# Slot attention with a split-precision feed-forward: laying the slot weights' maxima along the rows by two DMAs through device memory

## The chip, the cores and the metric

The kernel runs on one core of a Trainium2 chip. The metric is the device time of one execution in microseconds (us); lower is better. A core has TensorE (PE; PEld is its weight loads), VectorE (DVE), ScalarE (ACT), GpSimd (POOL) and SyncE (SP), each with an in-order queue of its own, and DMA engines that move data for all of them. SyncE issues all of this kernel's DMAs.

## The reference

Eight batches of eight heads, 576 positions, head size 64, 32 memory slots. A softmax of phi along the positions gives the slot weights, these sum k and v into 32 slots, q attends to the slots, and a feed-forward with an exact gelu follows.

```python
a = phi - np.max(phi, axis=2, keepdims=True)
a = np.exp(a)
a = a / (np.sum(a, axis=2, keepdims=True) + 1e-09)
k_m = np.einsum('bhsm,bhsd->bhmd', a, k)
v_m = np.einsum('bhsm,bhsd->bhmd', a, v)
scores = scale * np.matmul(q, k_m.transpose(0, 1, 3, 2))
...
attn_out = np.matmul(attn, v_m)
...
h = x @ w_in
g = 0.5 * h * (1.0 + erf(h * inv_sqrt2))
return g @ w_out
```

x is the attention's output, 4608 rows of 512; w_in is 512 by 2048, w_out 2048 by 512. Everything is float32.

## The kernel before

**The main stream.** Slots times w_in are folded first: per batch, U = (v slots) times w_in (pu, L441), so that the hidden layer of a batch is h = U times the attention weights. The 2048 hidden units go in 16 slices f of 128. For each slice of a batch TensorE makes h in two halves of 288 positions (L680, 12 products in the trace), ACT applies gelu from PSUM (gf, L690 for the first half; L692 and tails, L693, for the second), DVE splits gf into a high part gh and a rest gl (L155, L699), and TensorE projects with w_out (L712, three products for each of four accumulators, 12 products). The projection of a slice stands in TensorE's queue behind h of the next slice. h lives in two PSUM banks, one for each half, so the next slice's half waits for gelu of the same half. A step is one half. Batches 0 and 1 run slices 0 to 7, then 8 to 15, by turns; batches 2 to 7 run all 16 at once. After each odd batch the last 64 positions of two batches are projected together (tacc).

**The preparation of a batch** is laid between these steps, far ahead. For batch b from 2 on it needs the slot weights in two layouts. With slots on the partitions phi is loaded (Lphi, L240), DVE takes the maxima along the positions, negated (nm, L292, two columns of 128 values), and ACT makes the exponentials only for their sums (L298). With positions on the partitions phi is loaded again as aT (Lphin, L335 for 512 positions and L340 for the last 64). Here the maxima are needed along the free axis, the same row on every partition. The old way is a diagonal matrix (dg, L348: the identity times the column nm) and a product of ones with it (L355), which leaves in PSUM the row of maxima on every partition; for batches 2 and 3 in a pair of banks of its own, pn, for later ones in a free half of the pair tn that holds the transposes of the last batch's slots (L407). Then DVE adds the row to aT (L362) and ACT takes exponentials in place (L366, the 64 positions and the 512 apart). The products of aT with k and v (pk or psc, L383) give the slots, five position pieces for each of two head groups, each piece with its own kv load (L251, eight buffers). km (L397) scales them, L407 transposes, kT is copied by ACT, and score and pu follow (L441).

**What sets the order.** The first part up to batch 1 is written out by hand (START). From there `put(t, ...)` gives pieces a step at which they are due, and the program's scheduler reorders each engine's queue under the rule that a piece comes no earlier than four steps ahead of its due time. `prepare(b, t, tn)` sets the due steps: phi's load at t, the maxima at t + 2, the diagonal at t + 3, the load of aT at tn - 1, sums and exponentials at tn + 1. The pair of PSUM banks (pool ps_at, one buffer) is shared by pn, tn, pk, psc and pu; the next one waits until the readers of the last are done. ACT's exponential and gelu are in different tables, and each change of table is a load.

Of the kernel before, what the change touches and what calls it, by code (L numbers as in the profile page):

```python
# [9 lines left out]
F32 = mybir.dt.float32  # L10
# [4 lines left out]
ALU = mybir.AluOpType  # L15
# [57 lines left out]
def slot_attention_gelu_ffn(  # L73
# [28 lines left out]
    nc = tc.nc  # L102
    P = 128
    B, G, _, S = phiT.shape
# [19 lines left out]
    const = ctx.enter_context(tc.tile_pool(name="const", bufs=1))  # L124
    gs = ctx.enter_context(tc.tile_pool(name="gs", bufs=2))
    sb = ctx.enter_context(tc.tile_pool(name="sb", bufs=2))
    ps_acc = ctx.enter_context(tc.tile_pool(name="ps_acc", bufs=1, space=bass.MemoryType.PSUM))
    ps_h = ctx.enter_context(tc.tile_pool(name="ps_h", bufs=2, space=bass.MemoryType.PSUM))
    ps_at = ctx.enter_context(tc.tile_pool(name="ps_at", bufs=1, space=bass.MemoryType.PSUM))
# [4 lines left out]
    ones = one.to_broadcast([P, P])  # L134
    ident = const.tile([P, P], F32, name="ident")
# [12 lines left out]
    st = {"engine": None}  # L148
# [10 lines left out]
    def tile_of(key, make):  # L159
        if key not in st:  # L160
            st[key] = make()
        return st[key]

    def banks(*k):

        return tile_of(
            k, lambda: ps_at.tile([P, G, FB], F32, tag="at", name="_".join(map(str, k)))
        )
# [10 lines left out]
    def load_w(k, f):  # L179
        at = slice(f * P, (f + 1) * P)  # L180
        if k == 0:
            i = nc.sync.dma_start(
                raw_of(f)[:, 0].rearrange("p (c n) t -> p c (n t)", c=ND),
                w_in[:, at].bitcast(I32).rearrange("(c p) n -> p c n", p=P),
            )
        else:
            i = nc.sync.dma_start(
                raw_of(f)[:, 1].rearrange("p n t -> p (n t)"), w_out[at, :].bitcast(I32)
            )

        if "gate" in st:
            tc.add_manual_dep(i.ins, st["gate"].ins.name, edge, reason="U first")
# [148 lines left out]
            aT[P - TL :, full].rearrange("p g n -> p (g n)"), phiN[b, full * P :]  # L341
        )

    def a_diag(b):

        dg = st["dg", b] = sb.tile([P, G, P], F32, tag="dg", name=f"dg_{b}", bufs=1)
        for g in range(G):
            nc.vector.tensor_scalar_mul(dg[:, g], ident, st["nm", b][:, g : g + 1])  # L348

    def a_cols(b):  # L350

        pn = banks("tn", b - 1) if b > 3 else banks("pn", b)
        pn = st["pn", b] = pn[:, 1, : G * P].rearrange("p (g n) -> p g n", g=G)
        for g in range(G):
            nc.tensor.matmul(pn[:, g], ones, st["dg", b][:, g], start=True, stop=True)  # L355

    def a_nat(b):

        aT, pn, full = st["aT", b], st["pn", b], S // P
        xs = ((aT[P - TL :, full:], P - TL, 1), (aT[:, :full], 0, full))  # L360
        for x, r, n in xs:
            nc.vector.tensor_tensor(  # L362
                x, x, pn[r:].unsqueeze(1).to_broadcast([P - r, n, G, P]), op=ALU.add
            )
        for x, _, _ in xs:
            nc.scalar.activation(x, x, AF.Exp)  # L366
# [392 lines left out]
    def tail_evict(b):  # L759
# [7 lines left out]
    pieces = {  # L767
        "Lphi": load_phi, "Lkv": load_kv, "Lkv0": load_kv0, "Lq": load_q,
        "Lwi": lambda f: load_w(0, f), "Lwo": lambda f: load_w(1, f),
        "Lphin": load_phin, "dg": a_diag, "pn": a_cols, "anat": a_nat, "amax": a_max, "aexp": a_exp, "anorm": a_norm,  # L770
        "at": a_T, "atc": a_Tc, "slots": slots, "km": slots_m,
        "slotsT": slots_T, "kT": k_T,
        "n_score": score_n, "n_max": n_max, "n_sub": n_sub, "n_exp": n_exp, "n_sum": n_sum,
# [23 lines left out]
    def put(t, *xs):  # L797
        for x in xs:
            if x not in done:
                plan.append((t, len(plan), x))  # L800
# [6 lines left out]
    n = 2 * NF  # L807

    def prepare(b, t, tn):

        put(t, *(f"Lphi.{b}.{g}" for g in range(G)))
        put(t + 2, *(f"amax.{b}.{g}" for g in range(G)))
        put(t + 3, f"dg.{b}")
        put(tn - 1, f"Lphin.{b}")

        put(tn + 1, f"anat.{b}", *(f"aexp.{b}.{g}" for g in range(G)), f"anorm.{b}")


    for b, t in ((2, T2), (3, 65)):
        prepare(b, t, t + 5)  # L820
        put(t + 1, *(f"Lkv.{b}.0.{c}" for c in range(NC)))
        put(t + 5, f"pn.{b}")
        put(t + 9, f"slots.{b}.0", f"km.{b}.0")
        put(t + 9, *(f"Lkv.{b}.1.{c}" for c in range(NC)))
        put(t + 11, f"slots.{b}.1", f"km.{b}.1")
# [3 lines left out]
    for b in range(3, B):  # L829
        t = n * (b - 1)  # L830
        tn = {3: 78, 4: 91}.get(b, t - n + 24)
        put(tn, f"slotsT.{b}")
        if b + 1 < B:
            prepare(b + 1, tn - 8, tn)
            put(tn, f"pn.{b + 1}")
        put(tn, f"kT.{b}")
    for b in range(2, B):
        t = n * (b - 1)
# [17 lines left out]
    for f in range(NF):  # L856
        t = 2 * at_step[0, f]
# [86 lines left out]
```

## Time and profile before

| | |
|---|---|
| Time, median of 3 runs | 734.56 us (734.01 to 736.58) |
| Span of the profiled execution, first to last instruction | 733.8 us |
| Chain that ended last: TensorE's share | 90% |
| L355 products in the trace | 24 (12 in the program), 3.6 us busy |
| L348 diagonals on DVE | 12, 3.1 us busy |
| ACT table loads in the groups L298, L366, L571, L690, L692 | 12, 8, 13, 30, 4 at 1.28 us |
| DMA | 65.15 MB, 26.5% of the engines' time |

The profiled execution's span lies 0.2 us under the fastest run and 0.8 us under the median, so the two can be laid side by side to within about a microsecond. In the trace each float32 product of the program is two instructions. A row of the chain gives a start, a length and what the time went to; a row of a timeline gives start, length, engine, line, operation and tiles, with the idle time before it and what ended it in brackets. Batch numbers count from 0.

### The profile page before, as it was taken

The numbers are of one execution on the slowest core, as the hardware profiler recorded it, in microseconds if no ns is written. First come the engines' busy times: TensorE is split into PE (matmuls) and PEld (weight loads), VectorE is DVE, ScalarE is ACT, GpSimd is POOL, SyncE is SP. The second block draws the span as 40 slices with busy tenths as digits, with TensorE's granted clock in tenths as the row PEclk, the third lists the DMA queues.
The fourth block names the chain that finished last, engine by engine and source line by source line (L and its number), as shares of the span: only waits on it lengthen the run. The fifth ranks groups of instructions, "written<-read, shape, count | busy, mean of one in ns | idle before, by whom it ended". The sixth has DMA issues, their size and how long they took to land.

```text
span 733.8 us, 12179 instructions
## 1 busy us (share of the span) xinstructions
PE 708.0 (96%) x4958; PEld 578.8 (79%) x4958; DVE 394.7 (54%) x686; ACT 346.6 (47%) x713; POOL 48.7 (7%) x45
## 2 busy tenths in 40 slices
PE   5888899999999999999999999999999999999997
PEld 4666687886788887888888878888788888888886
DVE  2799999844674347535454364533643346333323
ACT  4577886782427847524752247432431234232210
POOL 1043243300000000000000000000000000000000
PEclk7589999999999999999999999999999999999999
DMA  9964163305432433051101521050101110010002
GB/s 296 320 213 140 58 220 104 120 1 187 137 105 71 150 112 95 23 216 62 33 1 59 193 62 33 1 205 25 37 1 59 47 33 1 0 58 1 1 1 72
DMA packets 42584, 65.15 MB, mean 89 GB/s; under 512 B 2848, under 2 KB 24992, under 8 KB 42528
## 3 DMA queue, kind: packets, MB, share of 16 engines
q1 hardware_dynamic: 42528, 64.37, 26.5%
q8 instruction: 39, 0.64, 0.4%
q14 instruction: 17, 0.14, 0.1%
HBM read 54.92 MB, written 9.44 MB: 88 GB/s over the span
## 4 chain that ended last, share of the span: by engine, by line
PE 90%; DVE 3%; ACT 2%; issue 2%; DMA 1%; SPq 0%; POOL 0%; ACTq 0%; POOLq 0%
PE acc L712 47%; PE h L680 27%; PE tacc L712 6%; PE pu L441 4%; PE psc L383 1%; DMA kv<-kv 1%; PE psc L441 1%; PE psc L458 1%; PE pk L383 1%; DVE raw L208 1%; DVE y L207 1%; DVE gl L699 0%; DVE s L482 0%; DVE wo_lo L230 0%; PE tn L355 0%
## 5 line engine op out<-in xcount | busy, mean ns | idle before, releaser
L680 PE MATMUL h<-p_hi,U 128*128 128x288 f32 x1024 | 206.4, 300 | 4.5 <-ACT tails L693 3.3
L712 PE MATMUL acc<-wo_hi,gh 128*128 128x512 f32 x512 | 203.0, 396 | 0.0
L712 PE MATMUL acc<-wo_lo,gh 128*128 128x512 f32 x512 | 201.2, 393 | 0.0
L712 PE MATMUL acc<-wo_hi,gl 128*128 128x512 f32 x512 | 201.0, 394 | 0.0
L680 PEld LDWEIGHTS h<-p_hi,U 128*128 128x128 f32 x1024 | 164.4, 189 | 26.0 <-issue 6.7
L690 ACT ACTIVATE gf<-h 128x288 f32<-128x288 f32 x128 | 52.9, 413 | 231.3 <-issue 167.7
L155 DVE CAST gh<-gf 128x512 fp32r<-128x512 f32 x108 | 46.7, 432 | 199.8 <-ACT gf L692 199.6
L712 PEld LDWEIGHTS acc<-wo_hi,gh 128*128 128x128 f32 x512 | 96.1, 188 | 33.2 <-DVE gh L155 7.5
L712 PEld LDWEIGHTS acc<-wo_hi,gl 128*128 128x128 f32 x512 | 95.9, 188 | 22.7 <-DVE gh L155 0.8
L680 PE MATMUL h<-p_lo,U 128*128 128x288 f32 x512 | 110.1, 296 | 0.4 <-DVE p_lo L536 0.4
L712 PEld LDWEIGHTS acc<-wo_lo,gh 128*128 128x128 f32 x512 | 96.1, 188 | 17.4 <-issue 0.4
L699 DVE TENSOR_TENSOR gl<-gf,gh 128x512 fp32r<-128x512 f32 x128 | 89.9, 703 | 10.1 <-ACT gh L155 1.6
L680 PEld LDWEIGHTS h<-p_lo,U 128*128 128x128 f32 x512 | 83.3, 189 | 1.8 <-DVE p_lo L536 1.0
L692 ACT ACTIVATE gf<-h 128x224 f32<-128x224 f32 x128 | 45.6, 356 | 41.9 <-PE h L680 41.8
L643 DVE TENSOR_TENSOR U<-pu,U 128x1024 fp32r<-128x1024 f32 (+2 forms) x39 | 40.0, 1024 | 14.9 <-ACT U L155 14.9
L690 ACT ACT_TABLE_LOAD x30 | 38.5, 1283 | 10.2 <-issue 6.3
L155 ACT CAST U<-pu 128x1024 fp32r<-128x1024 f32 (+2 forms) x39 | 33.8, 867 | 19.8 <-PE pu L441 19.8
L441 PE MATMUL pu<-w_in_sb,kT 64*32 64x512 f32 (+2 forms) x624 | 37.0, 531 | 2.5 <-DVE U L643 2.1
L208 DVE SCALAR_TENSOR_TENSOR raw<-raw 128x512 int32<-128x512 int32 (+1 forms) x33 | 36.4, 1104 | 0.3
L693 ACT ACTIVATE tails<-h 128x64 f32<-128x64 f32 x128 | 28.3, 221 | 0.0
L549 DVE STREAM_TRANSPOSE sT<-psc 128x288 f32<-128x288 f32 x28 | 12.1, 463 | 29.8 <-PE psc L383 24.2
L202 ACT ACTIVATE y<-raw 128x512 f32<-128x512 f32 (+1 forms) x33 | 22.9, 693 | 10.8 <-DMA raw<-w_in 7.0
(94 smaller groups left out, 625.8 us busy)
## 6 DMA issues: line engine op xcount, KB each, us to landing
kv<-kv SPq DMA_DIRECT2D x68, 256.0 KB, 4.5
raw<-w_in SPq DMA_DIRECT2D x16, 512.0 KB, 6.4
raw<-w_out SPq DMA_DIRECT2D x16, 512.0 KB, 6.5
out<-o SPq DMA_DIRECT2D x16, 512.0 KB, 2.9
q<-qT SPq DMA_DIRECT2D x14, 576.0 KB, 5.3
phi<-phiT SPq DMA_DIRECT2D x16, 288.0 KB, 5.5
aT<-phiN SPq DMA_DIRECT2D x6, 512.0 KB, 4.6
kv<-kv SPq DMA_DIRECT2D x4, 512.0 KB, 10.1
```

The lines of the kernel that those rows point to most:

```text
L155: return e.copy(dst, src) if e is nc.scalar else e.tensor_copy(dst, src)
L202: nc.scalar.activation(y, high.bitcast(F32), AF.Abs, scale=2.0**16)
L208: nc.vector.scalar_tensor_tensor(low, high, -(2**31), low, op0=ALU.bitwise_and, op1=ALU.bitwise_or)
L383: nc.tensor.matmul(pk[32 * j : 32 * j + 32, w0 * D : (w0 + n) * D], st["aT", b][:rows, c, g, 32 * j : 32 * j + 32], t[:rows, w0 : w0 + n, ...
L441: nc.tensor.matmul(ps[g][M * j : M * j + M], st["kT", b][rows, t, M * j : M * j + M], moving[rows, j, :], start=True, stop=True,)
L643: nc.vector.tensor_sub(u[:, :, 1], st["pu", b, f], u[:, :, 0].bitcast(F32))
L680: i = nc.tensor.matmul(h[:, :HS], u[g][w], x[:, g, :], start=(n == 0), stop=(n == 3 * G - 1))
L690: nc.scalar.activation(gf[:, :HS], h[:, :HS], AF.Gelu)
L692: nc.scalar.activation(gf[:, HS:], h[:, : MAIN - HS], AF.Gelu)
L693: nc.scalar.activation(tails()[:, f, b % 2], h[:, MAIN - HS : HS], AF.Gelu)
L699: nc.vector.tensor_tensor(g_of("gl", b, f), g_of("gf", b, f), g_of("gh", b, f).bitcast(F32), op=ALU.subtract)
L712: nc.tensor.matmul(acc, x, w[:, f, :], start=(first and n == 0), stop=(last and n == 2))
```

## The change

From batch 2 on the diagonal and the product are gone. The column nm is written by a DMA into a tile in device memory (row, two rows of 128), and a second DMA reads these rows back to every partition of a tile in SBUF (nb); DVE adds nb to aT. Both DMAs are issued by SyncE, and the second waits until the first has landed. The preparation of batches 2 and 3 starts one step earlier, and its aT load, sums and exponentials are due one step later.

```diff
+    hbm = ctx.enter_context(tc.tile_pool(name="hbm", bufs=2, space=bass.MemoryType.DRAM))
...
-    def a_diag(b):
-
-        dg = st["dg", b] = sb.tile([P, G, P], F32, tag="dg", name=f"dg_{b}", bufs=1)
-        for g in range(G):
-            nc.vector.tensor_scalar_mul(dg[:, g], ident, st["nm", b][:, g : g + 1])
-
-    def a_cols(b):
-
-        pn = banks("tn", b - 1) if b > 3 else banks("pn", b)
-        pn = st["pn", b] = pn[:, 1, : G * P].rearrange("p (g n) -> p g n", g=G)
-        for g in range(G):
-            nc.tensor.matmul(pn[:, g], ones, st["dg", b][:, g], start=True, stop=True)
+    def a_row(b):
+
+        row = hbm.tile([G, P], F32, tag="row", name=f"row_{b}")
+        nc.sync.dma_start(row.rearrange("g p -> p g"), st["nm", b])
+        nb = st["nb", b] = sb.tile([P, G, P], F32, tag="nb", name=f"nb_{b}", bufs=1)
+        nc.sync.dma_start(nb, row.unsqueeze(0).to_broadcast([P, G, P]))
 
     def a_nat(b):
 
-        aT, pn, full = st["aT", b], st["pn", b], S // P
+        aT, nb, full = st["aT", b], st["nb", b], S // P
...
-                x, x, pn[r:].unsqueeze(1).to_broadcast([P - r, n, G, P]), op=ALU.add
+                x, x, nb[r:].unsqueeze(1).to_broadcast([P - r, n, G, P]), op=ALU.add
...
-        put(t + 3, f"dg.{b}")
+        put(t + 3, f"row.{b}")
...
-        prepare(b, t, t + 5)
+        prepare(b, t - 1, t + 6)
...
-        put(t + 5, f"pn.{b}")
...
-            put(tn, f"pn.{b + 1}")
```

The scheduler lays the queues anew. Three places matter below; the last number of a name is a serial number, and lines of the new kernel differ by a few from the old.

On ACT, where batch 2 is prepared (slices 13 to 15 of batch 0), there stood before:

```order
L298 ACT_TABLE_LOAD
L298 ACTIVATE phi_1626,sm_1769<-phi_1626,nm_1684 128x576
L690 ACT_TABLE_LOAD
L690 ACTIVATE gf_14_1722<-h_0_14_1715 128x288
L692 ACTIVATE gf_14_1722<-h_1_14_1728 128x224
L693 ACTIVATE tails<-h_1_14_1728 128x64
L366 ACT_TABLE_LOAD
L366 ACTIVATE aT_1724<-aT_1724 64x256
L690 ACT_TABLE_LOAD
L690 ACTIVATE gf_15_1763<-h_0_15_1756 128x288
L366 ACT_TABLE_LOAD
L366 ACTIVATE aT_1724<-aT_1724 128x1024
```

and now stands:

```order
L361 ACT_TABLE_LOAD
L361 ACTIVATE aT_1740<-aT_1740 64x256
L685 ACT_TABLE_LOAD
L685 ACTIVATE gf_14_1725<-h_0_14_1718 128x288
L687 ACTIVATE gf_14_1725<-h_1_14_1727 128x224
L688 ACTIVATE tails<-h_1_14_1727 128x64
L361 ACT_TABLE_LOAD
L361 ACTIVATE aT_1740<-aT_1740 128x1024
L685 ACT_TABLE_LOAD
L685 ACTIVATE gf_15_1763<-h_0_15_1756 128x288
L687 ACTIVATE gf_15_1763<-h_1_15_1765 128x224
L688 ACTIVATE tails<-h_1_15_1765 128x64
```

The exponentials of aT have moved ahead by one slice and lie between slices; the second exponential of phi has moved behind slice 15. On DVE the two sums come ahead of gh and gl of slice 13, the 512 positions first. On SyncE the load of aT, which stood right behind phi's, stands behind row, and its tail behind nb.

On SyncE, between the last kv loads of batch 3 (kv_1_3, kv_1_4, numbers 25..) and the loads of batch 4, there stood before:

```order
L251 DMA kv_1_3_2584<-kv 128x512
L251 DMA kv_1_4_2586<-kv 128x512
L251 DMA kv_0_0_2661<-kv 128x512
L251 DMA kv_0_1_2663<-kv 128x512
L251 DMA kv_0_2_2665<-kv 128x512
L285 DMA q_0_2749<-qT 128x4x288
L251 DMA kv_0_3_2667<-kv 128x512
L335 DMA aT_2657<-phiN 128x4x256
```

and now stands:

```order
L241 DMA phi_2454<-phiT 128x576 x2
L252 DMA kv_1_3_2583<-kv 128x512
L348 DMA row_2517<-nm_2501 128x2x1
L252 DMA kv_1_4_2585<-kv 128x512
L252 DMA kv_0_0_2660<-kv 128x512
L252 DMA kv_0_1_2662<-kv 128x512
L350 DMA nb_2519<-row_2517 128x256
L252 DMA kv_0_2_2664<-kv 128x512
L336 DMA aT_2656<-phiN 128x4x256
```

Batch 4's phi, which was issued ahead of all five kv loads of batch 3's second group, now stands ahead of the fourth, row ahead of the fifth, and nb ahead of batch 4's aT. The second phi exponential of batch 3, whose end frees the tile for batch 4's phi, has moved on ACT behind both exponentials of aT and half of the next gelu. On TensorE the first group of five pieces (pk of batch 3) has moved from between the two halves of slice 5 to behind ten products of the projection that follows, and the second group is cut into four pieces and one.

On ACT, in batch 5's slices 11 to 13, where batch 6 is prepared, there stood before (from the copy of kT on):

```order
L155 COPY kT_3769<-tn_3764 128x256
L692 ACTIVATE gf_12_3762<-h_1_12_3771 128x224
L693 ACTIVATE tails<-h_1_12_3771 128x64
L155 CAST p_hi_1_3796<-pT_1_3794 128x576
L366 ACT_TABLE_LOAD
L366 ACTIVATE aT_3739<-aT_3739 64x256
L366 ACTIVATE aT_3739<-aT_3739 128x1024
L690 ACT_TABLE_LOAD
L690 ACTIVATE gf_13_3831<-h_0_13_3824 128x288
L155 CAST U_0_3809<-pu_0_3800 128x2x512
```

and now stands:

```order
L156 COPY kT_3764<-tn_3761 128x256
L361 ACT_TABLE_LOAD
L361 ACTIVATE aT_3736<-aT_3736 64x256
L687 ACT_TABLE_LOAD
L687 ACTIVATE gf_12_3759<-h_1_12_3766 128x224
L688 ACTIVATE tails<-h_1_12_3766 128x64
L361 ACT_TABLE_LOAD
L361 ACTIVATE aT_3736<-aT_3736 128x1024
L156 CAST p_hi_1_3791<-pT_1_3789 128x576
L156 CAST U_0_3804<-pu_0_3795 128x2x512
L685 ACT_TABLE_LOAD
L685 ACTIVATE gf_13_3826<-h_0_13_3819 128x288
```

The two exponentials are apart, with a pair of table loads more between them, and the cast of U has come ahead of slice 13's gelu. Batch 7 reads the same. On TensorE pu, which stood within slice 13's second h, now stands right behind slice 12's h, ahead of a projection, since the banks of tn no longer wait for DVE's sums.

More of the change, by code (lines that the diff above doesn't have):

```diff
@@ L769, in slot_attention_gelu_ffn @@
         "Lwi": lambda f: load_w(0, f), "Lwo": lambda f: load_w(1, f),
-        "Lphin": load_phin, "dg": a_diag, "pn": a_cols, "anat": a_nat, "amax": a_max, "aexp": a_exp, "anorm": a_norm,
+        "Lphin": load_phin, "row": a_row, "anat": a_nat, "amax": a_max, "aexp": a_exp, "anorm": a_norm,
         "at": a_T, "atc": a_Tc, "slots": slots, "km": slots_m,
```

## The prediction

> **What bounds the kernel now.** I read the page first, then the stages, then the chain of waits stage by stage, and last the timelines of ACT, DVE and SyncE's queue where the change puts its hands. The page's first part and the head of its chain:
>
> ```profile
> PE 708.0 (96%) x4958; PEld 578.8 (79%) x4958; DVE 394.7 (54%) x686; ACT 346.6 (47%) x713; POOL 48.7 (7%) x45
> ...
> PE 90%; DVE 3%; ACT 2%; issue 2%; DMA 1%; SPq 0%; POOL 0%; ACTq 0%; POOLq 0%
> ```
>
> The stage table (PE, PEld, DVE, ACT, POOL busy, clock, DMA share, GB/s) has this row for a stretch in which batches 3 and 4 are prepared:
>
> ```profile
> 240.00:310.00 70.00, 70.00 (x582) 56.79 (x581) 37.67 (x69) 46.26 (x79) 0.61 (x2) 1.00 0.27 88
> ```
>
> TensorE is the bound: never idle there, at full clock, and it carries nine tenths of the chain. So an edit counts by what it takes from TensorE's queue or what wait it puts into it; DVE, ACT and the DMA engines have room on average and matter only where TensorE is made to wait.
>
> Around batch 2's maxima the chain, in order of time (start, length, what), reads:
>
> ```profile
> 155.42 1.59 PE h L680 x12
> 157.01 0.44 PE pn L355 x4
> ...
> 161.82 2.77 PE acc L712 x12
> 164.58 0.81 PE h L680 x6
> ...
> 165.42 1.06 ACT L692
> ...
> 166.50 0.36 ACT gf L692
> ...
> 167.02 1.06 PE h L680 x6
> ```
>
> A slice takes 1.59 + 2.77 = 4.36 us on TensorE. The group pn, which the change deletes, lies on the path with 0.44. And there is one real wait: between 164.58 + 0.81 = 165.39 and 167.02 TensorE stands still, 1.6 us, for ACT, which is loading a table.
>
> **The deleted products.** The same chain in the other batches:
>
> ```profile
> 231.30 0.45 PE pn L355 x4
> ...
> 246.37 0.80 PE h L680 x6
> 247.17 1.23 PE pk L383 x40
> ...
> 252.91 1.23 PE pk L383 x40
> ...
> 258.88 0.45 PE tn L355 x4
> ```
>
> and in batches 6 and 7 (two answers):
>
> ```profile
> 366.12 0.46 PE tn L355 x4
> ...
> 366.63 0.36 ACT gf L692
> ...
> 367.15 1.06 PE h L680 x6
> ...
> 376.53 1.59 PE h L680 x12
> ```
>
> ```profile
> 457.19 0.46 PE tn L355 x4
> ...
> 457.69 0.36 ACT gf L692
> ```
>
> In batches 2 and 3 the group stands alone and goes whole: 0.44 + 0.45. In batches 4 and 5 it stands behind the transposes of L407, which stay, and with them the change from one kind of product to the other; I take 0.4 each. In batches 6 and 7 TensorE waits for ACT right behind the group (366.63 and 457.69): without the group it waits 0.46 longer, so nothing. Sum: **-1.7 us**. The diagonals (L348) and the sums with a row from SBUF in place of PSUM are DVE's, which is covered by TensorE; if that cover went, it would be a gain of some tenths a batch.
>
> **The wait at 165.4.** ACT there, as the timeline has it:
>
> ```profile
> 162.40 0.41 ACT L690 ACTIVATE gf<-h 128x288 f32<-128x288 f32 x1
> 162.83 1.28 ACT L366 ACT_TABLE_LOAD   x1
> 164.12 1.06 ACT L366 ACTIVATE aT<-aT 128x1024 f32<-128x1024 f32 x1
> 165.20 1.28 ACT L692 ACT_TABLE_LOAD   x1
> ```
>
> The exponential of aT with its two table loads (1.28 + 1.06 + 1.28 = 3.62) sits between the two halves of slice 15's gelu, and the next slice's second h needs the PSUM bank of the second half. In the new order it sits between slices, and the other exponential of phi goes behind slice 15's whole gelu: both halves are through by 163.2 (162.40 + 0.41 + 0.36) and TensorE wants the bank at 165.4. The displaced phi exponential (two loads and about 1 us) then ends near 166.7, and its gelu is wanted one slice later. **-1.6 us**, provided that DVE's sums come in time. That is the new wait in batch 2, since DVE runs in order and gh and gl of slice 13 stand behind the sums:
>
> ```profile
> 146.09 0.74 DVE L292 TENSOR_REDUCE nm<-phi 128x1 f32<-128x576 f32 x1
> ...
> 154.87 0.43 DVE L155 CAST gh<-gf 128x512 fp32r<-128x512 f32 x1 [2.96 <-ACT gf L692]
> 155.40 0.69 DVE L699 TENSOR_TENSOR gl<-gf,gh 128x512 fp32r<-128x512 f32 x1
> ```
>
> The maxima are there at 146.8. Then SyncE issues row, the large aT load, waits until row has landed (x), issues nb and the tail of aT. No row shows a write of 256 pieces of 4 bytes or a read of one kilobyte by 128 partitions; the nearest are the writes of 128 KB and the loads of 64 KB (KB each, median us to landing):
>
> ```profile
> out<-to SPq DMA_DIRECT2D x8, 128.0 KB, 2.4
> ...
> aT<-phiN SPq DMA_DIRECT2D x6, 64.0 KB, 4.4
> ```
>
> With x = 3, nearest to the write, the last load is issued near 150.5 and lands near 154.9; sum of the tail 0.4, gh 0.43, gl 0.69: 156.4. TensorE wants gl at 156.85 + 2 x 0.23 = 157.3 (three products of a slice's twelve in 2.77). Hidden, with 0.9 us to spare: 0, and one for one beyond x = 3.9. Below, x can't give a gain, since gh waits for gelu at 154.8 anyhow. By the Trainium skill, "DMA: Bandwidth & Descriptors", section "Rules for kernel authors", a strided last dimension becomes one descriptor per element, which speaks against this write. By the same page's section "Anatomy of one DMA" (for GpSimd's path) a small transfer costs about 2.0 us, mostly the write's receipt; with that for x the sum is the same. No run here shows either for this write.
>
> **The queue in batches 3 and 4.** ACT's second phi exponential of batch 3, which frees the tile for batch 4's phi, and how long those two loads take from issue:
>
> ```profile
> 233.15 0.78 ACT L298 ACTIVATE phi<-phi,nm 128x576 f32<-128x576 f32 x1
> ```
>
> ```profile
> DMA to landing us min/median/max: 2.8/3.0/3.1
> ```
>
> That exponential moves behind two more exponentials, two slices and a table load (2 x 4.36 + 1.28 = 10 us), to 243.2. So phi of batch 4 is issued at 244, has landed at 247.5, and its two maxima, with U's subtraction between them, are ready near 249.6. Row goes out behind the load before it, near 250.7, and behind row stands the last kv piece of batch 3, which in the old queue waits for no maximum. It lands 2.5 to 3.7 us later by the kv loads of batch 2:
>
> ```profile
> DMA to landing us min/median/max: 2.5/3.2/3.7
> ```
>
> that is at 253.7 to 254.9. On TensorE the first group of five pieces moves from between the two h to behind ten of the projection's twelve products (246.37 - 0.45 + 2 x 0.80 + 10 x 0.23 = 249.8). The second group, today at 252.91, is cut into four and one, and the one is reached near 254.1 (249.8 + 1.23, two products, a half h, four pieces, the bubbles and half of the next h). So 0 to 0.8 of waiting, I take 0.3, and 0.35 for one more change of the kind of product: **+0.65**. In batch 4 the aT load stands behind nb, which waits for row: issued near 250.7 + x + 0.9, landed about 4.4 later, then DVE's two sums (2.5 times the columns of gl, so 1.7), gh and gl, 2.8 in all: gl is there at 258.8 + x and wanted near 264.6, hidden up to x = 5.8. In batches 5 to 7 row and nb stand ahead of loads that TensorE releases much later, well before their use.
>
> **Batches 6 and 7.** ACT in batch 6 from the copy of kT on:
>
> ```profile
> 367.27 0.39 ACT L155 COPY kT<-tn 128x256 f32<-128x256 f32 x1
> 368.25 0.36 ACT L692 ACTIVATE gf<-h 128x224 f32<-128x224 f32 x1 [0.58 <-PE h L680]
> ...
> 368.61 0.68 ACT L155 CAST p_hi<-pT 128x576 fp32r<-128x576 f32 x1
> 369.30 1.28 ACT L366 ACT_TABLE_LOAD   x1
> 370.60 0.42 ACT L366 ACTIVATE aT<-aT 64x256 f32<-64x256 f32 x1
> 371.80 1.06 ACT L366 ACTIVATE aT<-aT 128x1024 f32<-128x1024 f32 x1 [0.79 <-DVE aT L362]
> ...
> 374.48 1.01 ACT L155 CAST U<-pu 128x1024 fp32r<-128x1024 f32 x1
> ```
>
> The new order has a pair of loads more here and the cast of U ahead of slice 13's gelu: 367.27 + 0.39 + 4 x 1.28 + 0.42 + 0.6 (gelu and tails) + 1.06 + 0.68 + 1.01 = 376.55, and 0.41 for gelu, 376.96. TensorE wants slice 14's h at 376.4 in the timeline, 376.5 with pu moved ahead of a projection: 0.45 of waiting and 0.1 for the move, **+0.55 in each, +1.1**. In batch 5 the same exponentials join another under one table and save a pair, off the path.
>
> **Sum.** -1.7 - 1.6 + 0.65 + 1.1 = -1.55. The profiled execution's span is 733.8; less 1.55 that is 732.2. The median of the runs, 734.56, lies 0.8 above the span, so **733.0 us**.
>
> **Rivals.** 0.5% is 3.7 us, about what a measurement of this kernel can tell from no change.
>
> Clean removal, 730.5 (0.16): no new wait in batches 3, 6 and 7, and the 0.46 of the last two is gained as well (-1.7 - 1.6 - 0.8 = -4.1). For it: ACT is idle over half the time and could run ahead. Against: the sum of ACT's pieces above.
>
> No gain, 735 (0.14): DVE's wait for the landing delays ACT's exponential in batch 2, so that the table wait only moves; -1.7 + 0.65 + 1.1 and some tenths more in batch 3. So the change would not do to the time what it does to the queue. For it: the spare 0.9 us is small.
>
> Slow trip through device memory, 739 (0.10): TensorE stands still behind gl in batch 2 and in batch 4. It decides from x = 3.9 in batch 2 and from x = 5.8 in batch 4; at x = 8 it costs 4.1 + 2.2, so -1.55 + 6.3 = +4.75, or 739; at x = 7 it is 737. The page's rule on 4-byte pieces would act here. Against it: 16 pieces to each of 16 engines are few, and all writes of the table land within 3.5 us.
>
> The forecast has 0.60. Faster by over 0.5% (under 730.9): most of the clean removal, 0.14; slower (over 738.2): most of the slow trip, 0.09; within 0.5%: 0.77. The range leaves out the ends of both: 730.2 to 737.4.
>
> **What would show it.** Right: no pn or tn from dg in the chain; no wait for ACT tails in batch 2; a wait of some tenths for ACT gf in batches 6 and 7; DVE's aT sums waiting for DMA nb or aT in batch 2 without TensorE behind them; row landing in 2 to 4 us. Wrong: TensorE waiting for DVE gh or gl near 157, for kv near 252 by more than 1 us, or for nothing at all in batches 6 and 7.

## The result: 2.5% slower

The changed kernel takes 754.16 us (median of 4 runs, 753.8 to 754.6) where the kernel before takes 735.57 beside it (4 runs): a ratio of 1.0251, 95% interval 1.0234 to 1.0267. That is 18.6 us, and 21 above the forecast. The profiled execution's span is 752.3, against 733.8.

The first part of the page of the changed kernel: TensorE is busy 4 us longer though it has fewer products; the two stages below show where from.

```profile
PE 712.1 (95%) x4934; PEld 579.5 (77%) x4934; DVE 393.1 (52%) x674; ACT 346.6 (46%) x713; POOL 47.6 (6%) x45
```

What TensorE waited for, and what SyncE's queue waited for, in the whole execution (total us, times, longest). Of the first, 8.0 us are new and fall in batch 3 (the kernel before waited 5.2 us for kv, all of it before 150 us); the second is new, and the third is the second DMA behind the first:

```profile
PE pk L378 <- DMA kv<-kv: 8.5, 3, 5.2
PE acc L707 <- DVE gh L156: 6.3, 1, 6.3
```

```profile
SPq L350 <- DMA row<-nm: 48.0, 6, 9.4
```

The stages (PE, PEld, DVE, ACT, POOL busy, clock, DMA share, GB/s): first 150 to 170 in the kernel before, then the changed kernel. Its second is the one shown in the prediction with TensorE busy for all 70.00 us at clock 1.00:

```profile
150.00:170.00 20.00, 18.36 (x103) 16.07 (x102) 8.55 (x18) 17.31 (x27) 0.03 (x1) 1.00 0.00 1
```

```profile
150.00:170.00 20.00, 13.71 (x68) 11.61 (x67) 6.29 (x9) 11.34 (x17) 0.83 (x1) 0.83 0.36 65
...
240.00:310.00 70.00, 61.07 (x504) 48.34 (x503) 29.97 (x55) 41.00 (x71) 0.61 (x2) 0.93 0.41 101
```

TensorE stands still in both, for 6.3 and 8.9 us, and the granted clock is 0.83 and 0.93 where it was 1.00. To place every microsecond I compare when the first product of the same slice's projection starts in two traces. Differences to the kernel before, in us, by stages of that kernel's time, for the changed kernel and four of the experiments below:

```
stage of before    work there      changed  e2 due times  e6 pairs  e13 blocks  e7 batch 2's due times
  0 to  73         start            +0.8       +1.1         -0.2       -0.3        +0.1
152 to 173         batch 2          +5.7       -1.5         -1.7       +1.2        -1.6
173 to 243         between          -1.0       -0.4         -0.7       -0.8        -0.2
243 to 281         batches 3, 4    +11.2       +0.8         +7.7       +1.5         0.0
281 to 331         batch 5          +0.8        0.0          0.0       +0.1         0.0
331 to 412         batch 6          +0.5        0.0         +0.5       +0.5         0.0
412 to 502         batch 7          +0.6        0.0         +0.5       +0.6         0.0
```

The change touches nothing in the first 73 us; what differs there, up to 1.2 us either way, is scatter of single executions. The loss is in two places.

**Batch 2.** SyncE's queue and the loads around row (KB each, us to landing):

```profile
147.66 0.38 SPq L348 DMA_DIRECT2D row<-nm  x1
148.09 0.47 SPq L336 DMA_DIRECT2D aT<-phiN  x1
156.21 0.34 SPq L350 DMA_DIRECT2D nb<-row  x1
```

```profile
aT<-phiN SPq DMA_DIRECT2D x1, 512.0 KB, 12.6
nb<-row SPq DMA_DIRECT2D x1, 128.0 KB, 5.6
...
row<-nm SPq DMA_DIRECT2D x1, 1.0 KB, 8.5
```

One kilobyte takes 8.5 us to land, and the load issued right behind it 12.6 where the median of these loads was 4.6 before. DVE's timeline shows the rest of the way, and TensorE's the end of it:

```profile
161.91 1.68 DVE L357 TENSOR_TENSOR aT<-aT,nb 128x1024 f32<-128x1024 f32 x2 [9.47 <-DMA nb<-row]
163.62 0.43 DVE L156 CAST gh<-gf 128x512 fp32r<-128x512 f32 x1
```

```profile
164.10 0.80 PE L707 MATMUL acc<-wo_hi,gh 128*128 128x512 f32 x1 [6.29 <-DVE gh L156]
164.69 0.63 PE L707 MATMUL acc<-wo_lo,gh 128*128 128x512 f32 x1
165.12 0.63 PE L707 MATMUL acc<-wo_hi,gl 128*128 128x512 f32 x1
...
167.65 0.39 PE L707 MATMUL acc<-wo_hi,gl 128*128 128x512 f32 x1
167.88 0.40 PE L707 MATMUL acc<-wo_hi,gh 128*128 128x512 f32 x1
```

gh's gelu, on ACT, was done long before:

```profile
155.28 0.35 ACT L687 ACTIVATE gf<-h 128x224 f32<-128x224 f32 x1
```

gh is late because it stands behind the sums in DVE's queue. And the wait costs more than its 6.29 us: the eight products after it start 0.43 us apart and more, the later ones 0.23. The stage table has the granted clock at half there:

```profile
164.10:167.60 3.50, 3.50 (x8) 2.71 (x9) 1.81 (x3) 3.46 (x6) 0.00 (x0) 0.50 0.00 0
```

So TensorE works at about half pace for 3.5 us, which is some 1.6 us more. With the table wait gone (-1.9 from one slice to the next) and the product gone (-0.44) that makes 5.5; measured 5.7.

**Batch 3.** TensorE's timeline among the five pieces of the second group, and the kv loads issued from 256.5 to 258.0, the last two of that group with row between them:

```profile
258.93 0.86 PE L378 MATMUL pk<-kv,aT 128*32 128x128 f32 x24
264.97 0.66 PE L378 MATMUL pk<-kv,aT 128*32 128x128 f32 x8 [5.17 <-DMA kv<-kv]
...
269.50 0.65 PE L378 MATMUL pk<-kv,aT 128*32 128x128 f32 x8 [2.86 <-DMA kv<-kv]
```

```profile
L252 SPq DMA_DIRECT2D kv<-kv x2: 328/866/1403, 256.7 to 257.6; - x2
...
DMA to landing us min/median/max: 8.2/10.0/11.8
```

The load that was issued ahead of row is late too. All five loads of that group in the kernel before:

```profile
L251 SPq DMA_DIRECT2D kv<-kv x5: 328/382/1199, 247.6 to 250.2; - x5
...
DMA to landing us min/median/max: 3.2/3.5/3.8
```

The waits are 8.0 us of this stage's 11.2. Most of the other 3 is half pace again: the granted clock is 0.50 for 10.2 us, in which TensorE is busy for 5.57, so that about 2.8 us more are spent than at full clock.

```profile
263.20:273.40 10.20, 5.57 (x28) 3.98 (x29) 1.47 (x3) 0.47 (x2) 0.30 (x1) 0.50 0.80 139
```

### The profile page after: what moved, and what is told of

Read it like the earlier page. It is cut to its first block, busy times and chain, and to the rows that moved or that the text cites. A ratio compares the mean times of both kernels' runs of the same rounds, so it can differ in the third digit from the quotient of the medians.

```text
span 752.3 us, 12154 instructions
## 1 busy us (share of the span) xinstructions
PE 712.1 (95%) x4934; PEld 579.5 (77%) x4934; DVE 393.1 (52%) x674; ACT 346.6 (46%) x713; POOL 47.6 (6%) x45
## 5 line engine op out<-in xcount | busy, mean ns | idle before, releaser
L378 PE MATMUL pk<-kv,aT 128*32 128x128 f32 (+2 forms) x368 | 14.3, 297 | 13.7 <-DMA kv<-kv 8.5
```

The costliest lines, as they stand in the source:

```text
L378: nc.tensor.matmul(pk[32 * j : 32 * j + 32, w0 * D : (w0 + n) * D], st["aT", b][:rows, c, g, 32 * j : 32 * j + 32], t[:rows, w0 : w0 + n, ...
```

## The experiments

Theory: row's write is slow by its layout in device memory, and loads around it are held up as long; TensorE pays where it waits for one of them. Rivals: the new order of the instructions costs the time (the order); SyncE's queue, which carries row and all the loads, makes it slow (the queue); any trip through device memory beside loads is as slow (the trip).

### The order without the DMAs (e2_schedule)

```diff
-        prepare(b, t, t + 5)
+        prepare(b, t - 1, t + 6)
...
-        put(t + 5, f"pn.{b}")
+        put(t + 6, f"pn.{b}")
```

> The kernel before, with its diagonal and its products, but with the new due times of batches 2 and 3 (everything one step earlier at the front and one later at the end). ACT has the new order there: the exponentials of aT between slices in batch 2, batch 4's phi issued late in batch 3. No DMA through device memory. Theory (the DMAs cost the time): 733 to 736, about the kernel before, with the table wait of batch 2 (1.6 us) gone and some tenths given back in batch 3. Rival (the new order costs the time): 745 or more, with TensorE waiting for kv near 252.

Measured: 735.24, ratio 0.9992 (0.9979 to 1.0005). Batch 2 gains 1.5 us and batch 3 gives 0.8 back, as the table shows. (From one slice to the next the steps are 1.9 and 1.5; two of the expectations below use these.) TensorE waits for no kv between 230 and 300. The order is out: alone it costs nothing.

### Row on another engine's queue (e4_act_row)

```diff
-        nc.sync.dma_start(row.rearrange("g p -> p g"), st["nm", b])
+        nc.scalar.dma_start(row.rearrange("g p -> p g"), st["nm", b])
```

> The changed kernel with row issued by ScalarE's DMA queue in place of SyncE's; nb and all loads stay on SyncE's. If row's 4-byte writes are slow by themselves: row still lands in 8 to 10 us and TensorE still waits about 6 us behind gh in batch 2. Then, if they hold up only what stands behind them in their own queue, the kv loads of batch 3 land in 3 to 4 us, TensorE's 8 us of waiting there goes and the time is about 743; if they hold up the loads of any queue, the kv loads still take 8 us or more and the time stays near 754. Rival (SyncE's queue makes row slow): row lands in 2 to 3 us and the time is near 736.

Measured: 753.32, ratio 1.0247 (1.0222 to 1.0271). Row's landings in this kernel, then those of the three kv loads issued at 257.0 to 257.9, which now have no row in their queue:

```profile
L348 ACTq DMA_DIRECT2D row<-nm x6: 366/366/402, 148.0 to 446.8; - x6
...
DMA to landing us min/median/max: 7.8/8.9/11.3
```

```profile
L252 SPq DMA_DIRECT2D kv<-kv x3: 328/378/1560, 257.0 to 257.9; - x3
...
DMA to landing us min/median/max: 6.8/10.0/10.7
```

A few other instructions change places with this edit, but the losses stand where they stood. The queue is out: row is as slow, and it holds up the loads of another queue about as long. The Trainium skill, "DMA: Bandwidth & Descriptors", section "Issuing engines are not separate DMA queues", says that all issuers' DMAs run on the same 16 engines and interleave; this trace agrees, with 6.8 to 10.7 us for loads that took 3.2 to 3.8.

### The write measured by itself (e1_prices, e8_prices)

Six writes in each, late in the kernel before, each from a fresh copy so that it starts there; the core of three of those in e8_prices:

```diff
+        if k == "A":
+            d = hbm.tile([2, P], F32, tag=name, name=name)
+            nc.sync.dma_start(d.rearrange("g p -> p g"), c[:, :2])
+        if k == "I":
+            d = hbm.tile([P, 2], F32, tag=name, name=name)
+            nc.sync.dma_start(d, c[:, 0:4:2])
+        if k == "M":
+            d = hbm.tile([P, 2], F32, tag=name, name=name)
+            nc.sync.dma_start(d, c[:, :2])
```

> The kernel before with six extra writes late in batches 6 and 7, where SyncE has almost nothing else to do; each reads a fresh copy of a few columns of gf and nobody reads its target. In the order of time: (A) 256 pieces of 4 bytes into one kilobyte of device memory, as row is written; (C) 128 pieces of 8 bytes into the same size; (D) the 4-byte pieces again, but into one row of SBUF, as two DMAs of 128; (B) 256 pieces of 4 bytes into device memory, each 64 bytes from the next; (E) two pieces of 512 bytes; (H) as A, with a kv load of 256 KB issued right behind. Theory (small writes to device memory are slow): A 8 to 10 us from issue to landing as in the changed kernel, C about half or a little more, D and E 2 to 3, and the kv load of H 8 us or more in place of 3.2. Rival (row was slow because of what SyncE's queue carried around it): A alone lands in 2 to 3 us, like E, and H's load in 3 to 4. If it is the common kilobyte that makes A slow, B is far faster than A; if it is the count of pieces, B is like A. The time itself stays within 2 us of before.

> The kernel before with six extra writes to device memory, late in batches 6 and 7, at places where SyncE has nothing else; nobody reads their targets. In the order of time: (A) row's own write, 256 pieces of 4 bytes in one kilobyte, where neighbouring partitions are 4 bytes apart; (I) 256 pieces of 4 bytes in one kilobyte, but the two of a partition side by side, so that the eight partitions that follow each other fill 64 bytes; (J) 128 pieces of 8 bytes, shifted by 32 bytes, so that each 64 bytes are filled by two such groups of eight; (K) 256 pieces of 4 bytes, neighbouring partitions 8 bytes apart; (L) 128 pieces of 4 bytes next to each other; (M) 128 pieces of 8 bytes as in the kernel with pairs. If the size of a piece makes it slow: A, I and K 8 us or more, L 4 to 5, J and M near 2.8. If it is 64 bytes that two of the DMA engines fill between them: A, J and L slow, I, K and M 2 to 3 us. If it is the number of pieces in the same kilobyte: A and I slow, the others 2 to 4.

The issues of e1_prices (KB each, us to landing; kv_probe is the load behind H; A and E have no landing in the record):

```profile
kv_probe<-kv SPq DMA_DIRECT2D x1, 256.0 KB, 10.8
probe_D<-c_D SPq DMA_DIRECT2D x2, 0.5 KB, 2.1
probe_C<-c_C SPq DMA_DIRECT2D x1, 1.0 KB, 2.8
probe_B<-c_B SPq DMA_DIRECT2D x1, 1.0 KB, 2.0
...
probe_H<-c_H SPq DMA_DIRECT2D x1, 1.0 KB, 11.0
```

and of e8_prices:

```profile
probe_A<-c_A SPq DMA_DIRECT2D x1, 1.0 KB, 8.3
probe_I<-c_I SPq DMA_DIRECT2D x1, 1.0 KB, 7.3
probe_J<-c_J SPq DMA_DIRECT2D x1, 1.0 KB, 3.7
probe_K<-c_K SPq DMA_DIRECT2D x1, 1.0 KB, 2.9
probe_L<-c_L SPq DMA_DIRECT2D x1, 0.5 KB, 7.3
probe_M<-c_M SPq DMA_DIRECT2D x1, 1.0 KB, 4.1
```

With nothing beside it, row's write still takes 8.3 us (A), and a lone kv load behind it 10.8 (H). Each was taken once, and the same write took 2.8 as C and 4.1 as M, so only the gap between 4.1 and 7.3 is read here. None of the three guesses in the second expectation holds. Not the size of a piece: 4-byte pieces 8 bytes apart (K) or 64 apart (B) land in 2.9 and 2.0. Not 64 bytes filled by two groups: I has none and is slow, J has them and is not (if the targets begin at a multiple of 64 bytes, which the trace doesn't show). Not the number in a kilobyte: L has half of A's pieces and is about as slow. What A, I and L have in common, and no quick one, is that two pieces of 4 bytes fall into the same 8 bytes of device memory; I and M write the same bytes to the same places, in 256 pieces and in 128. But A, I and L are also the only ones with 16 pieces in each 64 bytes (C, J, K and M have 8, B has 1), and no run tells the one reading from the other. Into SBUF the same pieces (D) take 2.1. The time is not spent in moving the pieces: A's DMA packets all lie within 1.2 us of its issue, K's too, and no packet of any DMA is in the trace in the 7 us that then pass before A counts as landed. Which part of the memory system does this the trace does not show, and it stays open. Both kernels' times stay at that of before (735.5 and 734.12, one run each, beside 734.88 and 736.05), since nothing waits there.

### Row as pairs (e6_pairs)

```diff
-        row = hbm.tile([G, P], F32, tag="row", name=f"row_{b}")
-        nc.sync.dma_start(row.rearrange("g p -> p g"), st["nm", b])
-        nb = st["nb", b] = sb.tile([P, G, P], F32, tag="nb", name=f"nb_{b}", bufs=1)
-        nc.sync.dma_start(nb, row.unsqueeze(0).to_broadcast([P, G, P]))
+        row = hbm.tile([P, G], F32, tag="row", name=f"row_{b}")
+        nc.sync.dma_start(row, st["nm", b])
+        nb = st["nb", b] = sb.tile([P, P, G], F32, tag="nb", name=f"nb_{b}", bufs=1)
+        nc.sync.dma_start(nb, row.unsqueeze(0).to_broadcast([P, P, G]))
...
-        aT, nb, full = st["aT", b], st["nb", b], S // P
+        aT, nb, full = st["aT", b], st["nb", b].rearrange("q n g -> q g n"), S // P
```

> The changed kernel with one thing other: row lies in device memory as 128 pairs (both maxima of a partition side by side), so its write has 128 pieces of 8 bytes in place of 256 of 4, and DVE reads nb with a stride of two. Every queue has the same instructions in the same order. Theory (the layout of row's write is what costs): row lands in about 2.8 us as the eight-byte write did alone, the loads beside it in 3 to 6, no wait of 6 us for gh in batch 2 nor for kv in batch 3, and the time is 733 to 737: the sum of the prediction for x = 3, with up to 2 us for what the later batches were seen to give back. Rival (a trip through device memory beside loads is slow in any layout): row still 6 us or more and the time 745 or more.

Measured: 741.66, ratio 1.0074 (1.0061 to 1.0087). The queues are alike instruction by instruction, so the layout (with DVE's reading of nb by a stride of two) made about 70% of the loss (from 1.0251 to 1.0074). TensorE's wait for gh in batch 2 is down to 0.2 us. But row's landing, and that of the last two kv loads of batch 3 around it, read:

```profile
L348 SPq DMA_DIRECT2D row<-nm x6: 326/356/1173, 146.6 to 437.8; - x6
...
DMA to landing us min/median/max: 2.7/4.3/6.6
```

```profile
L252 SPq DMA_DIRECT2D kv<-kv x2: 328/355/382, 248.8 to 250.5; - x2
...
DMA to landing us min/median/max: 5.4/5.9/6.4
```

That lies between theory and the trip: eight-byte pieces beside loads still hold them up, by some 2 to 3 us, and TensorE waits 4.0 us for kv there.

### Row as eight pieces of 128 bytes (e13_blocks)

The core of the edit; nm lies here in a tile of 32 columns (nm32), the rest of which GpSimd fills with zeros.

```diff
-        row = hbm.tile([G, P], F32, tag="row", name=f"row_{b}")
-        nc.sync.dma_start(row.rearrange("g p -> p g"), st["nm", b])
-        nb = st["nb", b] = sb.tile([P, G, P], F32, tag="nb", name=f"nb_{b}", bufs=1)
+        row = hbm.tile([G, P], F32, tag="row", name=f"row_{b}")
+        nb = st["nb", b] = sb.tile([P, G, P], F32, tag="nb", name=f"nb_{b}", bufs=1)
+        nc.vector.transpose(nb[:, 0, :M], st["nm32", b])
+        for g in range(G):
+            nc.sync.dma_start(row[g].rearrange("(i j) -> i j", j=M), nb[g::M, 0, :M])
```

> The changed kernel, with the two columns of maxima first turned by DVE in blocks of 32 by 32 (one short transpose a batch), so that row is written as eight pieces of 128 bytes by two DMAs in place of 256 pieces of 4 bytes by one. Due times as in the changed kernel; the queues are the same but for these instructions, for nb and the tail of aT changing places in batch 2, and for one piece of batch 3's slots that TensorE takes a product or two later. Theory (pieces of 4 or 8 bytes that lie next to each other are slow to land and hold up the loads around them): row lands in 2 to 3 us, the last kv loads of batch 3 in 3 to 4.5 us though row stands between them, batch 2 has no wait for gh, and the time is 735 to 738: the two microseconds gained in batch 2 against what batches 3 and 5 to 7 give back. Rival (any write to device memory beside those loads holds them up): row lands fast, but the kv loads take 5 to 7 us as with pairs, and the time is 740 to 742.

Measured: 737.57, ratio 1.0022 (1.0012 to 1.0033). What SyncE waited for row, in this kernel and in that with pairs (48.0 in the changed one):

```profile
SPq L360 <- DMA row<-nb: 9.2, 5, 3.2
```

```profile
SPq L350 <- DMA row<-nm: 21.1, 6, 6.2
```

and, in this one, the kv load issued ahead of row in batch 3, which had taken 8.2 us (the one behind row takes 3.8 as well), and what TensorE waited for between 150 and 290:

```profile
L252 SPq DMA_DIRECT2D kv<-kv x1: 327/327/327, 251.4 to 251.4; - x1
...
DMA to landing us min/median/max: 3.8/3.8/3.8
```

```profile
PE acc L717 <- DVE gh L156: 1.5, 1, 1.5
PE pk L388 <- DMA kv<-kv: 0.9, 2, 0.8
```

The trip is out, and with it nb's read of one kilobyte by all partitions: the same way, beside the same loads, in pieces that are not small, costs little. One expectation failed: batch 2 still waits 1.5 us for gh. DVE shows why: the maxima are there at 146.5, but the transpose stands behind a cast to gh and runs only at 149.89, so row is issued at 150.12. The granted clock then is 0.51 from 159.2 to 162.6, which makes the 1.5 us a loss of about 3 and turns the stage's gain of 1.5 into +1.2.

### Row behind the loads (e12_four_bytes_row4_late, e10_row4_late)

```diff
-        put(t + 3, f"row.{b}")
+        put(t + 3 + 4 * (b == 4), f"row.{b}")
```

> The changed kernel, 4-byte pieces and all, with batch 4's row due four steps later: on SyncE's queue it stands behind the last kv load of batch 3 in place of ahead of it. Theory (a row among the loads holds them up, before it and behind it in the queue): both last kv loads of batch 3 land 3 to 4 us after issue, TensorE's waits of 5.2 and 2.9 us go, and batch 3 costs at most the 1.5 us that the new due times alone cost there: about 745, with batch 2's wait of 6.3 us for gh untouched. Rival (the kv loads are late because phi of batch 4 is late): no change, 753 to 754.

> The kernel with pairs (8-byte pieces) with batch 4's row due four steps later, as in the kernel above. Theory: the kv loads of batch 3 that took 5.4 and 6.4 us land in 3 to 4, TensorE's 4 us of waiting there go but for about 1, and the time falls from 741.7 by 5 or 6 to about 736, the kernel before. Rival (late phi, not row): 741.

Measured: 751.66, ratio 1.0217 (1.0198 to 1.0237), and 740.21, ratio 1.0055 (1.0034 to 1.0076). With 4-byte pieces the two kv loads, now ahead of row, land as hoped:

```profile
L252 SPq DMA_DIRECT2D kv<-kv x2: 328/909/1490, 255.3 to 255.8; - x2
...
DMA to landing us min/median/max: 3.1/3.4/3.8
```

So row, not the late phi, had held them up. But the time fell by 2.5 us and not by 9; TensorE between 150 and 290, and DVE, show where the wait went:

```profile
PE acc L707 <- DVE gh L156: 12.5, 2, 6.7
PE pk L378 <- DMA kv<-kv: 0.7, 1, 0.7
```

```profile
274.61 1.68 DVE L357 TENSOR_TENSOR aT<-aT,nb 128x1024 f32<-128x1024 f32 x2 [12.00 <-DMA aT<-phiN]
```

Batch 4's sums run at the same time as in the changed kernel (274.6 and 274.7), where TensorE's wait for kv had covered them; now they make gh late as in batch 2. With pairs the last kv load, although issued 1.3 us ahead of row, still takes 5.7 us, and 3.1 of TensorE's 4.0 us of waiting stay.

### Where the DMAs cost little, and what is faster (e5, e7, e9, e11)

Row and nb for batches 5 to 7 only, the core of the edit:

```diff
-        put(t + 3, f"dg.{b}")
+        put(t + 3, f"row.{b}" if b > 4 else f"dg.{b}")
```

> Row and nb only for batches 5, 6 and 7; batches 2 to 4 keep diagonal, products and old due times. Theory (the loss is TensorE's waiting in batches 2 and 3): 736 to 738, that is before plus 0.5 in each of batches 6 and 7 and nothing else, although each row still takes 9 us to land. Rival (a row costs the same wherever it is): half of the 18.6 us, about 745.

Measured: 737.15, ratio 1.0023 (1.0009 to 1.0037); rows take 7.5 to 10.3 us and no engine waits for them; batches 6 and 7 give 0.5 each, batch 5 0.2.

The kernel before with the new due times for batch 2 alone:

```diff
-        prepare(b, t, t + 5)
+        prepare(b, t - (b == 2), t + 5 + (b == 2))
...
-        put(t + 5, f"pn.{b}")
+        put(t + 5 + (b == 2), f"pn.{b}")
```

> The kernel before, products and all, with the new due times for batch 2 alone. The kernel with the new due times for batches 2 and 3 gained 1.9 us in batch 2 and gave 1.5 back in batch 3. Theory (the wait between the halves of slice 15 is a matter of the order alone): 1.5 to 2 us faster than before, 733.0 to 733.5 beside 734.9. Rival (the gain needs the column off TensorE): no difference.

Measured: 734.14 beside 736.05, ratio 0.9973 (0.9963 to 0.9984). This is 0.3% faster than the kernel before, with the products in place. The two that add pairs to it, for batch 2 (`if b < 3`), and for batches 2 and 3 (`if b < 4`):

> As the kernel above, but batch 2 alone has row and nb. Expected: 1.9 + 0.44 = 2.3 us faster than before. Rival: with row in place of the product DVE's sums come so late that the table wait comes back, and it is no faster than before.

> Row and nb, in pairs, for batches 2 and 3 alone, with the new due times for batch 2 alone; batches 4 to 7 keep diagonal and products. No row then stands among loads that TensorE waits for. Expected: the gain of the new due times for batch 2 (1.9) and the products of batches 2 and 3 (0.44 + 0.45), less a few tenths for one more change of the kind of product in batch 3: about 2.5 us faster than before. If a write beside loads costs in batch 3 as well: no faster than the kernel with the new due times for batch 2 and products.

Measured: 734.62, ratio 0.9986 (0.9975 to 0.9997), and 734.76, ratio 0.9988 (0.9977 to 1.0000). Neither gains what was expected: 0.8 and 0.7 us. In batch 2's stage the traces with and without its product differ by 0.06 us (-1.58 and -1.64), not by 0.44: without it TensorE comes to the projection earlier and waits there 0.2 us for gh, which stands behind the sums. With batch 3's row the pieces of its slots move in TensorE's order and that stage loses 0.7.

## Why the prediction was wrong

The forecast of 733.0 (730.2 to 737.4) failed at two steps. The first is **x, the landing of row, taken as 3 us**, "nearest to the write" of 128 KB. It is 8.5 to 9.9 in the changed kernel and 8.3 alone. The distance in bytes from the nearest rows said nothing; the pieces were what differed, and no row of before bounds that. The second is **the loads around row, priced as if row were not there**: 2.5 to 3.7 us for kv behind row, 4.4 for nb and the load of aT behind it. Next to row kv took 8.2 and 11.8 us, the large aT load 12.6 (median 4.6 before), and nb 5.6. Nor did any term allow for the half pace behind a long wait. By the prediction's own prices x = 8.5 alone gives about 740; the second step and the half pace make the rest.

By the Trainium skill's figure for the fixed cost ("DMA: Bandwidth & Descriptors", section "Anatomy of one DMA", for GpSimd's path) x would have been 2.0. B and D come near it (2.0 and 2.1), the other quick layouts take 2.8 to 4.1, and row's own does not agree.

Point by point:

- **Batch 2, "hidden up to x = 3.9".** The mechanism was right: DVE's sums ahead of gh of slice 13. The price at x = 8 was given as 4.1; it is 6.3, since x is 8.5, nb itself takes 5.6 where 4.4 was taken, and both sums stand behind it (1.68 where 0.4 was taken). What the sum left out is TensorE's half pace afterwards, 1.6 more.
- **Batch 3, "it lands 2.5 to 3.7 us later by the kv loads".** This is the larger error: +0.65 was forecast, +11.2 came (it covers batch 4's part of that stretch too). The order was read rightly (row between the last two kv loads) but row was priced as a neighbour without effect. It holds up the loads ahead of it and behind it: 8.2 and 11.8 us. The part that is the order's own was sized well: the new due times alone give +0.8 there, without a wait for kv. That 0.35 of it is a change of the kind of product no row shows.
- **The slow trip, 0.10.** It is the rival that came nearest, with 739 for x = 8, but it had TensorE wait in batches 2 and 4 and not for kv in batch 3, which cost most. (That wait was named among the signs of being wrong, and both signs came.) Batch 4's part lay behind batch 3's wait until e12 uncovered it. The argument against it ("16 pieces to each of 16 engines are few") counted pieces, and e8's L shows that the count is not it. The Trainium skill's rule on strided last dimensions ("DMA: Bandwidth & Descriptors", section "Rules for kernel authors") spoke against this write, and so did the time; but it makes K as many pieces as A, and K lands in 2.9.
- **The table wait, -1.6.** It goes in every trace with the new due times: 1.9 from one slice to the next, after a loss of some 0.3 in the slice before. But it belongs to the due times, which e7 shows without any DMA.
- **The products, -1.7.** Batch 2's gives 0.06 in place of 0.44, since the gap was filled by a wait for gh. The others were not tried apart.
- **Batches 6 and 7, +0.55 each.** Measured +0.5 to +0.6 in every kernel that has row there: TensorE waits 0.3 us for gf, as said, and 1.0 for tails where it waited 0.6. Batch 5 was said to be off the path; it costs 0 to 1.3.
- **The step from span to run, 0.8.** It compared two different executions. In every run the time is 1.7 to 1.9 above its own span, so the level of the forecast was 1 us low; that is within the scatter and is not what failed.

## What to carry to other kernels

Before small columns are sent through device memory, look at how the pieces of the write lie: 4-byte pieces side by side took 7 to 11 us here and slowed the loads near them, so that the price is paid by whoever waits for those loads and not only by the reader of the row. Turn the columns into rows on an engine first, or keep the product, which was the faster of the two here by 0.2%. And if an edit comes with new due times, try the due times alone: here they held the whole gain.

## What was not expected of the hardware

- 4-byte pieces of one DMA side by side in device memory (two in the same 8 bytes): 7.3 to 8.3 us to land alone; 8 bytes apart 2.9, 64 apart 2.0, as 8-byte pieces 2.8 to 4.1, into SBUF 2.1. The packets are over within 1.5 us of issue; the rest passes after them.
- Such a write holds up loads of its own and of another queue, also one issued shortly ahead of it: 256 KB took 6.8 to 13.6 us in place of 3.2 to 3.8.
- Eight-byte pieces, 2.8 to 4.1 us alone, took up to 6.6 in the kernel and slowed the loads around them to 5.4 to 6.4.
- After a wait of 6.3 us TensorE's products started 0.43 us apart in place of 0.23 for 3.5 us, at a granted clock of 0.50. Behind a wait of 1.5 us in e13 the clock was 0.51 for 3.4 us; behind the wait of 1.6 us in the kernel before it stayed at 1.00. What decides between the two these runs do not show.
